# Float32 attention heads: exponential moved behind the transpose, maximum added in PSUM

## The chip, the cores and the metric

The kernel runs on one core of one Trainium2 chip. The metric is the device time of one execution in microseconds (us). Lower is better. Engines are named as in the profile: PE is TensorE's matmul stream, PEld its weight loads, DVE is VectorE, ACT is ScalarE, POOL is GpSimd, and SP issues most of the DMAs.

## What is computed

Attention for 8 batches of 8 heads (576 positions, 64 dimensions), followed by a gated feed-forward network over all 4608 tokens:

```
scores = scale * q @ k.T ; bias = -(cum[q] - cum[k]) with cum = cumsum(max(s, 0))
scores = where(causal, -1e9, scores + min(bias, 0))
scores = scores - max(scores) ; attn = exp(scores)
attn = attn / (sum(attn) + 1e-9) ; out = attn @ v
x = out as (4608, 512) ; gate = sigmoid(x @ w_gate) ; val = x @ w_val
y = (gate * val) @ w_out
```

q, k, v, s and the output are float32; the three weight matrices are float64.

## The kernel before

A head's 576 queries are cut into five tiles, numbered 0 to 4: tile 0 has 64 rows, the others 128, and tile t needs 64 + 128 t keys. A tile is one tick of the main loop, from tile 4 down to tile 0, so a head takes five ticks and there are 64 heads. The row maximum and the exponential work in two long SBUF buffers: `e_0` holds tiles 0, 1 and 2 (six blocks of 128 keys), `e_1` tiles 3 and 4 (nine blocks). There is one of each, so a tile of the next head may only be written when the same tile of this head has been read. The 64 columns behind a tile's keys are padding that later steps read.

The first eight heads (batch 0) run in float32 and their steps have names with `n_`. The other 56 run with operands split into two float16 parts (`s_part`, `max_part`, `p_part`, `av_part`) and have their probabilities transposed by DMA. A float32 tile goes through these steps:

- `n_s`: PE writes the scores to PSUM (L575), in two pieces for tile 4.
- `mask_part`: POOL masks the diagonal block in the bias row (L461).
- `n_max`: DVE adds the bias, negates, writes the sum to `e`, and takes the minimum (L584). The tile `em` receives it from an instruction that reads the accumulator. ACT then takes the exponential of the tile in place, from SBUF to SBUF, with `em` as bias (L587).
- `n_turn`: PE transposes blocks of `e` against the identity matrix, three to a PSUM bank `nt_ps` (L596). ACT copies each bank to the buffer `p16`, here used as float32 (L597). There are five banks to a head.
- `n_av`: PE multiplies the transposed probabilities by v and a column of ones (L605), DVE divides (L611 to L615), and after two heads `n_x` transposes the result (L629) and splits it into two float16 parts (L631, L632).

While these heads run, the feed-forward weights are prepared. A weight step takes 1024 values per partition of a float64 image (two 32-bit words each), decodes them (ACT L272, DVE L273, L274, L275), squares them (ACT L287), sums the squares over partitions (POOL L289), works out a power of two (DVE L125, L127), and writes high and low float16 parts (ACT L292, DVE L293). There are 18 such steps. The feed-forward matmuls (`ffn_in`, L657, and `ffn_out`, L687) start at tick 44 and go on, between the attention steps, until the end.

Each engine executes its own list in order. The lists are made by a scheduler with a timeline of its own; `first()` raises the priority of what it encloses. So an edit to one step also moves others in these lists.

Of the kernel before, what the change touches and what calls it, by code (L numbers as in the profile page):

```python
# [8 lines left out]
F32 = mybir.dt.float32  # L9
# [3 lines left out]
AF = mybir.ActivationFunctionType  # L13
ALU = mybir.AluOpType
ADD_REDUCE = bass.bass_isa.ReduceOp.add

P = 128
GT = 256
PSCALE = 2.0 ** 14
MASKED = 1.0e30  # L20
# [3 lines left out]
def tile_attention_then_gated_ffn(  # L24
# [11 lines left out]
    nc = tc.nc  # L36
# [10 lines left out]
    TILES = [(0, 64, 64)] + [(64 + 128 * i, 128, 192 + 128 * i) for i in range(4)]  # L47
    NTL = len(TILES)


    SETS = (((0, 1, 2), (0, 1, 3), 6), ((3, 4), (0, 4), 9))
    PAD = NTL * P - S
    NN = H
# [4 lines left out]
    wp = ctx.enter_context(tc.tile_pool(name="wp", bufs=2))  # L58
# [15 lines left out]
    e_s = [cp.tile([P, n * P], F32, name=f"e_{i}") for i, (_, _, n) in enumerate(SETS)]  # L74
# [4 lines left out]
    e_t, pf_t = {}, {}  # L79
# [3 lines left out]
            e_t[t] = e_s[i][:, cols]  # L83
            pf_t[t] = p_s[i].rearrange("p l n -> p (l n)").bitcast(F32)[:, cols]
    for t, (q0, m, w) in enumerate(TILES):
        nc.gpsimd.memset(e_t[t][:, w:], 0.0)
    ident = cp.tile([P, P], F32, name="ident")
    scrap = wp.tile([P, 2, NTL * P], F16, tag="x16", name="scrap", bufs=1).bitcast(F32)
    count, junk = scrap[:, 0, :P], scrap[:, 1, :P]
# [9 lines left out]
    for g in range(0, P, 32):  # L99
        nc.vector.tensor_scalar(ident[g : g + 32, g : g + 32], count[g : g + 32, :32], count[g : g + 32, 32:33], None,  # L100
                                ALU.is_equal)
    nc.gpsimd.memset(e_t[0][64:, :], 0.0)
    expo = cp.tile([P, 2], F32, name="expo")
    nc.gpsimd.memset(expo[:, 0:1], 460.75)
    nc.gpsimd.memset(expo[:, 1:2], 204.75)
# [13 lines left out]
    def first(now=True):  # L119
        return tc.high_priority(1000) if now else ExitStack()  # L120
# [355 lines left out]
    def p_part(i, h_):  # L476

        nc.scalar.activation(p_s[h_][:, 0], e_s[h_], AF.Copy, scale=PSCALE)  # L478
        ts, first_block, n = SETS[h_]
        flat = p_s[h_].rearrange("p l n -> p (l n)")  # L480
        for t, kb in zip(ts, first_block):
            if t:
                nc.vector.scalar_tensor_tensor(flat[:, LOW[t] * P : (LOW[t] + t) * P], e_t[t][:, : t * P], PSCALE,  # L483
                                               flat[:, kb * P : (kb + t) * P], ALU.mult, ALU.subtract)
        tails = [t + kb for t, kb in zip(ts, first_block)]
        e_ = e_s[h_].rearrange("p (b g n) -> p b g n", g=2, n=64)
        p_ = flat[:, : n * P].rearrange("p (b g n) -> p b g n", g=2, n=64)
        for bs in (tails[:2], tails[2:]):
            if bs:
                b = slice(bs[0], bs[-1] + 1, max(bs[-1] - bs[0], 1))  # L490
                nc.vector.scalar_tensor_tensor(p_[:, b, 1], e_[:, b, 0], PSCALE, p_[:, b, 0], ALU.mult, ALU.subtract)
        PT[i, h_] = wp.tile([P, 2 * n, P], F16, tag=f"pt{h_}", name=f"pt{h_}_{i}")
        m = n + sum(ts)
        nc.sync.dma_start_transpose(PT[i, h_][:, :m], flat[:, : m * P])
# [35 lines left out]
                                    x16.rearrange("p l n -> p (l n)"))  # L530


    qT, kT, nS, nA = {}, {}, {}, {}

    def n_load(p):
        b, h0 = divmod(2 * p, H)
# [39 lines left out]
            nS[i, t].append((ps, a, b_))  # L576

    def n_max(i, t):
        q0, m, w = TILES[t]
        init = MASKED  # L580
        r = rl[i]
        for n, (ps, a, b_) in enumerate(nS.pop((i, t))):
            acc = wp.tile([P, 1], F32, tag=f"em{n}", name=f"em{i}_{t}_{n}", bufs=3)
            nc.vector.tensor_tensor_reduce(e_t[t][:m, a:b_], ps[:m, : b_ - a], r[:m, a:b_], -1.0, init,  # L584
                                           ALU.add, ALU.min, acc[:m])
            init = acc[:m]
        nc.scalar.activation(e_t[t][:m, :w], e_t[t][:m, :w], AF.Exp, bias=init, scale=-1.0)  # L587

    def n_turn(i, t):

        h_, groups = {4: (1, (6,)), 3: (1, (3, 0)), 2: (0, (3,)), 1: (0, ()), 0: (0, (0,))}[t]
        o = p_s[h_].rearrange("p l n -> p (l n)").bitcast(F32)
        for a in groups:
            ps = pp.tile([P, 512], F32, tag="gv", name=f"nt_ps_{i}_{t}_{a}")
            for kb in range(3):
                nc.tensor.transpose(ps[:, kb * P : (kb + 1) * P], e_s[h_][:, (a + kb) * P : (a + kb + 1) * P], ident)  # L596
            nc.scalar.copy(o[:, a * P : (a + 3) * P], ps[:, : 3 * P])  # L597

    def n_av(i, t):
        p, j = divmod(i, 2)  # L600
# [140 lines left out]
    for n in range(nticks + 12):  # L741
        if n == NTL * EARLY:
            more_room()
        i, t = divmod(n, NTL)
# [10 lines left out]
        if 2 <= n < nticks + 2:  # L755
            a, z = divmod(n - 2, NTL)
            if a < NN:
                with first():
                    n_turn(a, NTL - 1 - z)
            elif z in (1, 4):  # L760
                p_part(a, 1 if z == 1 else 0)
        if 1 <= n < nticks + 1:
            a, z = divmod(n - 1, NTL)
            if a < NN:
                with first():
                    mask_part(a, NTL - 1 - z)
                    n_max(a, NTL - 1 - z)
            else:
                mask_part(a, NTL - 1 - z)
                max_part(a, NTL - 1 - z)  # L770
        if 3 <= n < 3 + NTL * NN:
            with first():
                a, z = divmod(n - 3, NTL)
# [113 lines left out]
        if n >= NE and state["u"] < 2 * NF:  # L887
            fdone = min(NF, int((n - NE + 1) * FPT))
            while state["u"] < 2 * fdone:
                f = state["u"]  # L890
# [17 lines left out]
        m = n - (11 if n > 2 * NTL * H + 30 else 7)  # L908
        b = m // (NTL * H) if m >= 0 else 0
        if b >= 1:  # L910
            r = m - b * NTL * H + 1
# [39 lines left out]
```

## Time and profile before

| | us |
|---|---|
| median of 3 runs | 1152.38 (1151.87 to 1155.03) |
| span of the profiled execution, first to last instruction | 1146.4 |
| what lies between that span and the median | 6.0 |
| PE busy over the span | 1091.6 (95%) |
| DVE busy | 776.1 (68%) |
| ACT busy | 749.5 (65%) |

The profiled execution shows its span but no time of its own; the median of the timed runs is put beside it instead. A busy time is the union of an engine's instructions, so shares of different engines overlap. The granted clock is the mean TensorE clock in a stretch, 1.00 being the higher of its two levels (2.4 GHz) and 0.50 the lower (1.2 GHz). A wait names the engine and line that ended the idle time before an instruction.

### The profile page before, as it was taken

What the parts mean: (1) busy time and instruction counts of PE and PEld (TensorE: products, weight loads), DVE (VectorE), ACT (ScalarE), POOL (GpSimd) and SP (SyncE); (2) the same over time, 40 slices, a digit from 0 to 9 for tenths busy, and PEclk for the clock granted to TensorE, in tenths of its full rate; (3) what the DMA queues carried; (4) which work ended last, traced back from release to release, by engine and by line L of the source; (5) the groups of instructions that cost most, each with busy time, mean ns of one, the idle gap of its engine ahead of it and who ended that gap; (6) DMA issues with size and microseconds to landing.
All of it is one profiled execution on the core that took longest, in us unless ns stands there. A gap on an engine that the chain in (4) does not pass through costs nothing.

```text
span 1146.4 us, 30336 instructions
## 1 busy us (share of the span) xinstructions
PE 1091.6 (95%) x11644; PEld 853.5 (74%) x11644; DVE 776.1 (68%) x2395; ACT 749.5 (65%) x1465; POOL 261.3 (23%) x568
## 2 busy tenths in 40 slices
PE   6787888989999999999999999999999999999998
PEld 4566676658767887788777777778877887787775
DVE  6899999866787777776565677777777775222222
ACT  6989778667777777676665577767776764233222
POOL 6634233222232222121211122212222221000000
PEclk9889899999999999999999999999999999999999
DMA  9676868995989888777646498868887774000000
GB/s 280 201 217 161 185 139 181 183 189 130 171 164 175 164 178 167 141 150 138 145 79 139 89 178 166 166 144 171 156 161 138 150 124 88 13 20 20 1 19 19
DMA packets 445518, 157.62 MB, mean 137 GB/s; under 512 B 403583, under 2 KB 435839, under 8 KB 445374
## 3 DMA queue, kind: packets, MB, share of 16 engines
q1 hardware_dynamic: 418686, 127.38, 57.6%
q10 hardware_dynamic: 23328, 17.04, 4.9%
q0 software_dynamic: 3360, 11.27, 3.0%
q8 instruction: 91, 1.49, 0.5%
q14 instruction: 53, 0.43, 0.1%
HBM read 56.92 MB, written 9.58 MB: 58 GB/s over the span
## 4 chain that ended last, share of the span: by engine, by line
PE 76%; DMA 7%; DVE 5%; issue 5%; ACT 5%; SPq 1%; POOL 1%; ACTq 0%; DVEq 0%; POOLq 0%
PE gv L657 42%; PE o L687 22%; PE s L447 3%; PE s L446 3%; DMA qk<-in_q_dram 1%; PE av L506 1%; PE av L508 1%; PE av L507 1%; DMA v<-in_v_dram 1%; DVE e L471 1%; PE s L575 1%; DMA pt<-p 1%; DMA T<-T 1%; PE na_ps L605 1%; DMA nqk<-in_q_dram 1%
## 5 line engine op out<-in xcount | busy, mean ns | idle before, releaser
L657 PE MATMUL gv<-x,w 128*128 128x256 f16 (+3 forms) x6912 | 613.2, 246 | 5.3 <-DVE t2f L664 2.7
L657 PEld LDWEIGHTS <-w 128*128 128x128 f16 x6912 | 533.8, 98 | 61.5 <-issue 5.2
L687 PE MATMUL o<-w2all,h 128*128 128x512 f16 x1296 | 314.8, 379 | 0.0
L461 POOL TENSOR_SCALAR_AFFINE_SELECT rl<-rl 128x64 f32<-128x64 f32 (+1 forms) x280 | 111.5, 399 | 519.7 <-DVE em L471 465.3
L474 ACT ACTIVATE e<-e,em 128x576 f32<-128x576 f32 x280 | 154.6, 554 | 92.3 <-DVE em L471 90.2
L687 PEld LDWEIGHTS <-h 128*128 128x128 f16 x1296 | 123.6, 98 | 108.7 <-issue 2.4
L662 ACT ACTIVATE th<-gv,scb 128x256 f32<-128x256 f32 (+3 forms) x288 | 111.4, 412 | 139.3 <-PE gv L657 138.4
L664 DVE SCALAR_TENSOR_TENSOR t<-th,gv 128x256 f32<-128x256 f32 x192 | 80.2, 417 | 133.5 <-ACT th L662 132.5
L471 DVE CUSTOM_DVE_ANT_0 e<-s,rl,qkcf 128x288 f32<-128x288 f32 x280 | 135.8, 485 | 30.5 <-PE s L447 24.9
L672 ACT ACTIVATE h<-t,hsc 128x256 f16<-128x256 f32 x192 | 96.6, 503 | 80.0 <-DVE t L664 80.0
L483 DVE SCALAR_TENSOR_TENSOR p<-e,p 128x384 f16<-128x384 f32 x224 | 102.0, 495 | 40.2 <-ACT p L478 39.4
L673 DVE SCALAR_TENSOR_TENSOR h<-t,hsc,h 128x256 f16<-128x256 f32 x192 | 93.2, 486 | 43.3 <-ACT h L672 42.8
L478 ACT ACTIVATE p<-e 128x1152 f16<-128x1152 f32 x112 | 112.1, 1001 | 2.8
L506 PE MATMUL av<-v,pt 128*128 128x65 f16 x560 | 68.0, 193 | 6.9 <-DMA pt<-p 6.9
L507 PE MATMUL av<-v,pt 128*128 128x64 f16 x560 | 68.0, 192 | 0.0
L446 PE MATMUL s<-T 128*128 128x288 f16 (+2 forms) x246 | 64.6, 280 | 3.6 <-DMA T<-qk 2.6
L508 PE MATMUL av<-v,pt 128*128 128x65 f16 x560 | 67.9, 194 | 0.0
L447 PE MATMUL s<-T 128*128 128x288 f16 (+2 forms) x246 | 62.2, 282 | 2.4 <-DMA T<-T 2.4
L506 PEld LDWEIGHTS <-pt 128*128 128x128 f16 x560 | 52.4, 97 | 13.6 <-DMA pt<-p 8.8
L706 POOL DMA_DIRECT2D out_dram<-osb x34 | 19.4, 570 | 174.6 <-ACT osb L705 173.8
L409 POOL PARTITION_BROADCAST cr<-cr x63 | 57.5, 913 | 6.1 <-DVE em L584 5.7
L455 DVE TENSOR_SCALAR rl<-cr,qkcf 128x576 f32<-128x576 f32 x56 | 29.1, 520 | 40.1 <-POOL cr L409 39.9
(157 smaller groups left out, 1436.9 us busy)
## 6 DMA issues: line engine op xcount, KB each, us to landing
v<-v SPq DMA_DIRECT2D x56, 162.5 KB
out_dram<-osb POOLq DMA_DIRECT2D x34, 256.0 KB, 2.9
v<-in_v_dram SPq DMA_DIRECT2D x64, 128.0 KB
T<-T SPq DMA_DIRECT2D x82, 72.0 KB
t2f<-in_v_dram SPq DMA_DIRECT2D x20, 288.0 KB
qk<-in_q_dram SPq DMA_DIRECT2D x17, 288.0 KB
qk<-in_k_dram SPq DMA_DIRECT2D x17, 288.0 KB
w2all<-in_moe_w_gate_dram ACTq DMA_DIRECT2D x7, 512.0 KB
```

The lines of the kernel that those rows point to most:

```text
L446: nc.tensor.matmul(ps[:, : b_ - a], lhs, T[i][:, 0, a:b_], start=True, stop=False)
L447: nc.tensor.matmul(ps[:, : b_ - a], lhs, T[i][:, 2, a:b_], start=False, stop=True)
L461: nc.gpsimd.affine_select(rl[i][:, q0:w], rl[i][:, q0:w], pattern=[[-1, m]], compare_op=ALU.is_ge, fill=-MASKED if i < NN else MASKED, bas ...
L471: nc.vector.tensor_tensor_reduce(e_t[t][:, a:b_], ps[:, : b_ - a], rl[i][:, a:b_], c, init, ALU.add, ALU.min, acc)
L474: nc.scalar.activation(e_t[t][:, :w], e_t[t][:, :w], AF.Exp, bias=init, scale=-1.0)
L478: nc.scalar.activation(p_s[h_][:, 0], e_s[h_], AF.Copy, scale=PSCALE)
L483: nc.vector.scalar_tensor_tensor(flat[:, LOW[t] * P : (LOW[t] + t) * P], e_t[t][:, : t * P], PSCALE, flat[:, kb * P : (kb + t) * P], ALU.m ...
L506: nc.tensor.matmul(AV[i][:, t], hi, v_[:, D : 2 * D + 1], start=kb == 0, stop=False)
L657: nc.tensor.matmul(ps[:, gv, a:e], w1[f][:, cc, gv, wl], x_of(b, cc)[:, xl, c0 + a : c0 + e], start=(c == 0), stop=(c == 3 * NC - 1))
L662: nc.scalar.activation(th[:, a:e], ps[:, 0, a:e], AF.Tanh, scale=scb[b][:, f : f + 1])
L672: nc.scalar.activation(h[:, 0], t2, AF.Copy, scale=hsc[:, f : f + 1])
L687: nc.tensor.matmul(ps[:m], h[:, hl, tt * P : tt * P + m], w2[f][:, wl], start=(f == 0 and c == 0), stop=(f == NF - 1 and c == 2))
```

## The change

In the float32 heads the sign is no longer turned while the bias is added: DVE takes the maximum of score plus bias over all 128 rows, and a further DVE instruction writes its negative to a tile `nm`. The in-place exponential is gone. PE transposes the block of raw sums and then, in the same PSUM group, adds a transposing matmul whose stationary operand is `nm` repeated over 128 columns, so that every column of the transposed block has its query's maximum subtracted. ACT then takes the exponential from PSUM where it copied before. The padding starts as minus 1e30, whose exponential is zero, and is set to zero after the last float32 head (`clear_pads`); the separate memset of the lower half of tile 0 goes.

```diff
-        nc.gpsimd.memset(e_t[t][:, w:], 0.0)
+        nc.gpsimd.memset(e_t[t][:, w:], -MASKED)
...
-    nc.gpsimd.memset(e_t[0][64:, :], 0.0)
...
+    tile_of = [[t for t, kb in zip(ts, first_block) for _ in range(t + 1)] for ts, first_block, _ in SETS]
+
+    def clear_pads():
+        for t, (q0, m, w) in enumerate(TILES):
+            nc.gpsimd.memset(e_t[t][:, w:], 0.0)
...
-        init = MASKED
+        init = -MASKED
...
-            nc.vector.tensor_tensor_reduce(e_t[t][:m, a:b_], ps[:m, : b_ - a], r[:m, a:b_], -1.0, init,
-                                           ALU.add, ALU.min, acc[:m])
-            init = acc[:m]
-        nc.scalar.activation(e_t[t][:m, :w], e_t[t][:m, :w], AF.Exp, bias=init, scale=-1.0)
+            nc.vector.tensor_tensor_reduce(e_t[t][:, a:b_], ps[:, : b_ - a], r[:, a:b_], 1.0, init,
+                                           ALU.add, ALU.max, acc)
+            init = acc
+        nmax[t] = wp.tile([P, 1], F32, tag="nm", name=f"nm{i}_{t}", bufs=4)
+        nc.vector.tensor_scalar(nmax[t], init, -1.0, None, ALU.mult)
...
-                nc.tensor.transpose(ps[:, kb * P : (kb + 1) * P], e_s[h_][:, (a + kb) * P : (a + kb + 1) * P], ident)
-            nc.scalar.copy(o[:, a * P : (a + 3) * P], ps[:, : 3 * P])
+                blk = ps[:, kb * P : (kb + 1) * P]
+                u = tile_of[h_][a + kb]
+                nc.tensor.matmul(blk, e_s[h_][:, (a + kb) * P : (a + kb + 1) * P], ident, start=True, stop=False,
+                                 is_transpose=True)
+                nc.tensor.matmul(blk, nmax[u].to_broadcast([P, P]), ident, start=False, stop=True, is_transpose=True)
+            nc.scalar.activation(o[:, a * P : (a + 3) * P], ps[:, : 3 * P], AF.Exp)
...
+                    if n == NTL * NN + 1:
+                        clear_pads()
```

The scheduler's lists change with it. On PE, the first transposes of head 1 (tile 4, bank `nt_ps_1_4_6`) stood together; the line numbers of the changed kernel are 4 to 8 higher here. Before:

```order
L575 MATMUL s1_0_0_432<-nk0_157,nq0_1_156 128x64
L596 MATMUL nt_ps_1_4_6_350<-ident_88,e_1_80 128x128 x3
L558 MATMUL nq_ps_1_1_1_391<-ident_88,nqk_1_229 128x96 x3
L596 MATMUL nt_ps_1_3_3_401<-ident_88,e_1_80 128x128 x3
L575 MATMUL s2_4_0_456<-nk1_371,nq1_0_369 128x288
```

The same place now:

```order
L602 MATMUL nt_ps_1_4_6_370<-ident_88,e_1_80 128x128
L579 MATMUL s1_1_0_423<-nk0_156,nq0_1_155 128x192
L604 MATMUL nt_ps_1_4_6_370<-ident_88,nm1_4_366 128x128
L602 MATMUL nt_ps_1_4_6_370<-ident_88,e_1_80 128x128
L604 MATMUL nt_ps_1_4_6_370<-ident_88,nm1_4_366 128x128
L602 MATMUL nt_ps_1_4_6_370<-ident_88,e_1_80 128x128
L604 MATMUL nt_ps_1_4_6_370<-ident_88,nm1_4_366 128x128
```

Each transpose is now followed by one that reads `nm`, and the group stands two score matmuls earlier in the list.

On DVE, the maximum of tile 4 of head 1 (two pieces, L584) and of tile 3 follow one another between weight steps (L293). Before:

```order
L584 ISA e_1_80,em1_4_1_345<-s1_4_288_309,cr1_186,em1_4_0_343 128x288
L584 ISA em1_4_1_345 128x1
L293 SCALAR_TENSOR_TENSOR w1_1_67<-w2all_78,wscale_111,w1_1_67 128x8x128
L584 ISA e_1_80,em1_3_0_358<-s1_3_0_333,cr1_186 128x448
L584 ISA em1_3_0_358 128x1
```

The same place now, where L273 is a weight step's instruction (L274 before):

```order
L587 ISA e_1_80,em1_3_0_381<-s1_3_0_349,cr1_185 128x448
L587 ISA em1_3_0_381 128x1
L273 SCALAR_TENSOR_TENSOR wa0_136<-wa0_136,w1_3_69 128x1024
L591 TENSOR_SCALAR nm1_3_383<-em1_3_0_381 128x1
L587 ISA e_0_79,em1_2_0_444<-s1_2_0_368,cr1_185 128x320
```

The negation stands not directly behind the maximum but behind one instruction of a weight step.

On ACT, the split of the first float16 head (`qk16_8`, whose transfer feeds head 8) stood among the exponentials of head 7. Before:

```order
L597 COPY p16_0_81<-nt_ps_6_2_3_1100 128x384
L587 ACTIVATE e_1_80<-e_1_80,em7_4_1_1156 128x576
L387 ACTIVATE qk16_8_1121<-qk32_4_981,qksc4_1092 96x6x64
L389 ACTIVATE qk16_8_1121<-qk32_4_981,qksc4_1092 96x6x64
L292 ACTIVATE w2all_78<-wa0_137,wscale_111 128x1024
```

The same pair now (L271 belongs to a weight step):

```order
L271 ACTIVATE wa0_136<-t2f_134 128x1024
L605 ACTIVATE p16_1_82<-nt_ps_6_3_0_1202 128x384
L386 ACTIVATE qk16_8_1256<-qk32_4_1097,qksc4_1223 96x6x64
L388 ACTIVATE qk16_8_1256<-qk32_4_1097,qksc4_1223 96x6x64
L605 ACTIVATE p16_0_81<-nt_ps_6_2_3_1231 128x384
```

It stands one bank of head 6 earlier, ahead of everything of head 7. From about the middle of head 18 on, the lists of all engines are the same as before.

## Rows read from the trace of the kernel before

**Rows 1.** Page, part 2: busy tenths in 40 slices of the span.

```profile
PE   6787888989999999999999999999999999999998
PEclk9889899999999999999999999999999999999999
```

**Rows 2.** Windows: busy us and instructions of each engine, granted clock, DMA share, GB/s.

```profile
200.00:300.00 100.00, 91.06 (x1059) 67.77 (x1058) 71.29 (x234) 67.87 (x135) 22.51 (x50) 1.00 0.86 170
300.00:600.00 300.00, 298.19 (x3534) 236.28 (x3532) 220.53 (x717) 212.17 (x423) 67.30 (x161) 1.00 0.76 150
600.00:900.00 300.00, 300.00 (x3289) 234.50 (x3287) 219.60 (x720) 208.04 (x404) 67.55 (x160) 1.00 0.77 150
```

**Rows 3.** Windows of the first 200 us: PE, PEld, DVE, ACT, POOL busy, clock.

```profile
20.00:66.00 46.00, 36.43 (x224) 29.70 (x223) 37.47 (x99) 44.52 (x90) 26.78 (x42) 0.83 0.78 235
66.00:110.00 44.00, 34.65 (x221) 26.54 (x219) 41.39 (x105) 40.32 (x74) 20.64 (x33) 0.97 0.66 179
110.00:120.00 10.00, 9.50 (x46) 7.92 (x45) 6.95 (x17) 5.92 (x12) 0.39 (x1) 0.52 0.64 144
120.00:200.00 80.00, 68.52 (x712) 55.69 (x709) 74.45 (x229) 65.13 (x120) 27.77 (x49) 0.98 0.84 173
```

**Rows 4.** Waits of DVE, 20 to 120 us: releaser, total us, times, longest.

```profile
DVE xe_w L125 <- POOL wtot L289: 4.9, 4, 2.4
DVE w L273 <- ACT w2all L272: 2.2, 2, 1.9
DVE w L293 <- ACT w L292: 1.2, 2, 1.0
DVE qk L388 <- ACT qk L387: 0.9, 1, 0.9
```

**Rows 5.** Waits of POOL, 20 to 120 us.

```profile
POOL wtot L289 <- ACT w2all L287: 9.4, 2, 7.9
POOL wtot L289 <- ACT w L287: 8.7, 7, 1.9
```

**Rows 6.** Groups on ACT, 0 to 130 us, then two forms: busy, mean ns | idle.

```profile
L587 ACT ACTIVATE e<-e,em 128x576 f32<-128x576 f32 (+4 forms) x40 | 22.1, 563 | 2.0 <-DVE em L584 1.9
L597 ACT COPY p<-nt_ps 128x384 f32<-128x384 f32 x40 | 18.4, 476 | 1.8 <-PE nt_ps L596 1.5 <-issue 0.3
...
L587 ACT ACTIVATE e<-e,em 128x448 f32<-128x448 f32 x8 | 5.4, 672 | 0.6 <-DVE em L584 0.6
L587 ACT ACTIVATE e<-e,em 128x320 f32<-128x320 f32 x8 | 4.6, 574 | 0.5 <-DVE em L584 0.5
```

**Rows 7.** DVE: forms (0 to 125 us), then two instructions in order of time.

```profile
L125 DVE TENSOR_SCALAR xe_w<-wtot 128x1 int32<-128x1 int32 x14 | 2.0, 146 | 5.2 <-POOL wtot L289 5.1
...
L584 DVE CUSTOM_DVE_ANT_0 e<-s,cr 128x192 f32<-128x192 f32 x8 | 2.8, 353 | 1.0 <-POOL cr L461 1.0
...
L584 DVE CUSTOM_DVE_ANT_0 e<-s,cr 64x64 f32<-64x64 f32 x8 | 1.7, 211 | 0.7 <-POOL cr L461 0.3
...
43.71 0.14 DVE L127 TENSOR_SCALAR wscale<-xe_w 128x1 int32<-128x1 int32 x1
43.77 0.51 DVE L584 CUSTOM_DVE_ANT_0 e<-s,cr,em 128x288 f32<-128x288 f32 x1
```

**Rows 8.** Timeline of PE: transposes at the higher and at the lower clock.

```profile
16.46 0.82 PE L596 MATMUL nt_ps<-ident,e 128*128 128x128 f32 x6
36.67 0.28 PE L596 MATMUL nt_ps<-ident,e 128*128 128x128 f32 x1
52.20 0.42 PE L596 MATMUL nt_ps<-ident,e 128*128 128x128 f32 x1
58.83 1.54 PE L596 MATMUL nt_ps<-ident,e 128*128 128x128 f32 x6 [0.70 <-ACT p L597]
```

**Rows 9.** Chain that ended last, first and last of four: start, us, what.

```profile
58.83 1.54 PE nt_ps L596 x6
...
65.07 1.08 PE s L575 x2
```

More of the change, by code (lines that the diff above doesn't have):

```diff
@@ L530, in split_x @@
                                     x16.rearrange("p l n -> p (l n)"))
-    qT, kT, nS, nA = {}, {}, {}, {}
+    qT, kT, nS, nA, nmax = {}, {}, {}, {}, {}
+    tile_of = [[t for t, kb in zip(ts, first_block) for _ in range(t + 1)] for ts, first_block, _ in SETS]
+    def clear_pads():
+        for t, (q0, m, w) in enumerate(TILES):
+            nc.gpsimd.memset(e_t[t][:, w:], 0.0)
     def n_load(p):
@@ L578, in n_max @@
     def n_max(i, t):
-        q0, m, w = TILES[t]
-        init = MASKED
+        init = -MASKED
         r = rl[i]
```

## The prediction

> **What bounds the kernel now.** I read the slices first, then the windows, the waits and the groups. From the seventh slice on PE is busy nine tenths or more [rows 1], 298 of 300 us and then 300 of 300 [rows 2]. There PE is the bound and runs the same list before and after. A microsecond gained or lost ahead of it goes through to the end; nothing else does. So what counts is how long the first 200 to 300 us take, and in those the float32 heads fill about 10 to 120.
>
> In 20 to 120 us, the first three of the windows in [rows 3], no engine is full all the time. ACT is busy 44.52 + 40.32 + 5.92 = 90.8 us, of which 20 to 66 is nearly solid (44.5 of 46). DVE is busy 85.8, with 14.2 idle, and is the tighter one from 66 to 110 (41.4 of 44). PE is busy 80.6, with 19.4 idle. From 120 to 200 DVE leads with 74.5 of 80. I take DVE as the ruler, since it is close to full before and after 120, and ask which of its gaps the change can close. Its waits [rows 4] say which end on ACT: 2.2 and 1.2 directly, 0.9 for head 8's split, and 4.9 through POOL's sum over partitions, which itself waits 8.7 + 9.4 us for ACT's squares [rows 5]. That is 9.2 of the 14.2 us.
>
> **The change part by part.**
>
> *ACT.* It loses 40 exponentials, 22.1 us busy [rows 6]. The 40 copies of 476 ns become 40 exponentials of 384 columns from PSUM, which no row shows. Lower bound: the copy's 476 ns, plus 0. Upper bound: the old exponential with its `em` operand, between its 320 and 448 column forms, (574 + 672) / 2 = 623 ns, 5.9 us in all. I take a quarter, 1.5 us, since shape, source and destination are the copy's and the operand `em` is gone. ACT goes from 90.8 to about 70 us in the stretch.
>
> *DVE.* It gains 40 instructions on 128x1. Such a one shows 146 ns, but the next starts 0.06 us after it [rows 7]. So 40 cost between 2.4 and 5.8 us; as the stream around them is dense, I take 0.075 each, 3.0 us. Tile 0's eight maxima now cover 128 rows: between 0 and 1.1 us (8 x 0.142, the step to the next form in [rows 7]); taken as 0, as the columns stay. The negation stands behind one weight instruction and PE waits for it there. Behind that wait stand score matmuls of the next tiles. Before, the transposes waited for an exponential in ACT's full list, so I add nothing.
>
> *PE.* It gains 120 transposes with weight loads. At the higher clock six take 0.82 us and one alone 0.28, so one more costs (0.82 - 0.28) / 5 = 0.108 us; at the lower, (1.54 - 0.42) / 5 = 0.224 us [rows 8]. That bounds the sum at 13.0 and 26.9 us. The granted clock, weighted over the three windows, is 0.86 [rows 3], so 28% of the stretch lies at 0.50; the mean cost is 0.14 and the sum 16.9 us. It goes into 19.4 us of PE idle time. I cost it at nothing on the path; the cover is 2.5 us thin, and what lies beyond it is the third case below.
>
> The rows show transposes at both clocks, in runs where other matmuls stand around them, and can't say whether a transpose helps to raise the clock. The Trainium skill, on its page "TensorE: Matmul & The Clock Gate", Part 4, says that transpose mode doesn't count as PE-busy in the same way and that the full clock doesn't engage for it. By that the added work would cost its upper bound; by the rows' mixture it costs the middle value. No row here settles it.
>
> *POOL.* One memset goes and five small ones move behind head 7. In 110 to 120 us POOL is busy 0.39 us [rows 3]; the float16 steps of head 8 that read the padding come later in every list. Cost 0, as that idle time hides them.
>
> *Order.* Head 8's split stands earlier on ACT, ahead of all of head 7, so its transfer starts earlier; the 0.9 us wait on it is in the 9.2.
>
> *Sum.* ACT sheds more than 20 us where DVE lost 9.2 us to it. A shorter list does not close every gap: the first one of 2.4 us also holds POOL's sum. Bounds are 0 and 9.2; I take five sixths, 7.7 us. Less 3.0 for the negations this leaves 4.7 us. Against the profiled execution that is a span of 1146.4 - 4.7 = 1141.7; with the 6.0 us that lie between its span and the median, 1147.7.
>
> **The rivals.**
>
> *PE takes ACT's place.* After the change PE is busy about 97.5 of 100 us in the stretch if the stretch keeps its length. In-order lists seldom reach that: DVE would then wait for scores as it waited for ACT. Against it: the transposes stand where PE waited anyway. Recovered 3.0, paid 3.0: 1152.4.
>
> *The transposes run at the lower clock.* If they draw the clock down, or leave it down as in 110 to 120 us (0.52), they cost 26.9 us, and PE's idle time holds only 19.4. It decides from 0.162 us for each (19.4 / 120), above the 0.14 of the mixture. The excess is 7.5 us; DVE's share is hidden under it: 1159.9. The page's rule above would lead here. For it: PE already ran at 0.83 in 20 to 66 with fewer transposes. Against it: six transposes ran at the higher clock at 16.46 us, and 66 to 110 kept 0.97 with just as many to a head.
>
> *The clock comes up.* From 58.83 to 66.15 the chain lies on PE at the lower clock [rows 9]. If denser PE work keeps it at the higher, half of these 7.3 us goes too: 4.7 + 3.7 = 8.4 less, 1144.0.
>
> **How the numbers follow.** A difference under 0.3%, 3.5 us, can't be told from none here. Forecast 0.42, with a range of its own from 1145.5 to 1150 that follows from recovering 9.2 or 5.4 us; PE in ACT's place 0.28; lower clock 0.22; higher clock 0.08. The edge of 0.3% is 1148.9, which leaves 0.08 of the forecast on the side of no change. So faster 0.34 + 0.08 = 0.42, same 0.08 + 0.28 = 0.36, slower 0.22. The range from 1143 to 1159 takes in the three likelier cases but for the upper half of the lower-clock case, and most of the fourth.
>
> **What would show it.** On ACT, the line of the in-place exponential is gone and the 40 from PSUM have a mean between 476 and 623 ns. DVE's 40 negations add about 3 us of busy time. The waits of DVE for ACT and for POOL's sum in the head stretch fall from 9.2 to about 2 us, and no wait of DVE for PE of like size appears. PE's busy time in the stretch rises by about 17 us and its idle time falls to a few. Head 8's first maximum comes some 5 us earlier, and the lag stays the same to the end. I am wrong if the added transposes have a spacing above 0.16 us, if DVE waits for scores, or if the gain is there at 120 us and is lost by 250, where transfers and PE meet.

## The result

| | median us | range, executions | mean granted clock (median) |
|---|---|---|---|
| before | 1153.87 | 1151.87 to 1155.60, 5 | 0.979 to 0.981 (beside the experiments) |
| changed | 1158.71 | 1156.42 to 1159.28, 5 | 0.984 |

The ratio is 1.0043, interval 1.0029 to 1.0058: about 5 us slower. Run again beside the last experiments, the changed kernel came to 1.0054 (1.0035 to 1.0073). The forecast was 1147.7, faster. Every ratio below is to the kernel before, run beside the experiment.

Single executions of one kernel differ by several us (before: 1146.98 to 1160.23 over 30 executions), so a profile is one draw. Below, sums and verdicts go by medians and ratios; profiles show where things stand.

### The profile page after: what moved, and what is told of

It reads as the page before. It is cut to its first block, busy times and chain, and to the rows that moved or that the text cites. A ratio compares the mean times of both kernels' runs of the same rounds, so it can differ in the third digit from the quotient of the medians.

```text
span 1156.9 us, 30566 instructions
## 1 busy us (share of the span) xinstructions
PE 1104.2 (95%) x11764; PEld 866.6 (75%) x11764; DVE 778.6 (67%) x2435; ACT 732.4 (63%) x1425; POOL 266.6 (23%) x572
## 4 chain that ended last, share of the span: by engine, by line
PE 80%; DMA 7%; DVE 4%; issue 3%; ACT 2%; POOL 1%; SPq 1%; DVEq 0%; ACTq 0%; POOLq 0%
PE gv L665 44%; PE o L695 23%; PE s L446 3%; PE s L445 3%; DMA qk<-in_q_dram 1%; PE av L507 1%; PE av L505 1%; DMA v<-in_v_dram 1%; PE av L506 1%; PE na_ps L613 1%; PE s L579 1%; DMA T<-T 1%; DMA w2all<-in_moe_w_val_dram 1%; DMA T<-qk 1%; PE av L509 1%
## 5 line engine op out<-in xcount | busy, mean ns | idle before, releaser
L695 PE MATMUL o<-w2all,h 128*128 128x512 f16 x1296 | 314.8, 379 | 0.8 <-ACT h L680 0.8
L460 POOL TENSOR_SCALAR_AFFINE_SELECT rl<-rl 128x64 f32<-128x64 f32 (+1 forms) x280 | 114.7, 411 | 544.5 <-DVE em L470 488.6
L695 PEld LDWEIGHTS <-h 128*128 128x128 f16 x1296 | 123.0, 98 | 106.8 <-ACT h L680 1.0
L470 DVE CUSTOM_DVE_ANT_0 e<-s,rl,qkcf 128x288 f32<-128x288 f32 x280 | 135.7, 486 | 30.4 <-PE s L446 25.7
L445 PE MATMUL s<-T 128*128 128x288 f16 (+2 forms) x246 | 65.5, 281 | 4.7 <-DVE em L470 4.5
L446 PE MATMUL s<-T 128*128 128x288 f16 (+2 forms) x246 | 63.9, 281 | 5.5 <-DMA T<-T 5.4
L505 PEld LDWEIGHTS <-pt 128*128 128x128 f16 x560 | 52.6, 98 | 11.0 <-DMA pt<-p 5.9
L506 PEld LDWEIGHTS <-pt 128*128 128x128 f16 x560 | 52.7, 97 | 4.9
```

The lines of the kernel that those rows point to most:

```text
L445: nc.tensor.matmul(ps[:, : b_ - a], lhs, T[i][:, 0, a:b_], start=True, stop=False)
L446: nc.tensor.matmul(ps[:, : b_ - a], lhs, T[i][:, 2, a:b_], start=False, stop=True)
L460: nc.gpsimd.affine_select(rl[i][:, q0:w], rl[i][:, q0:w], pattern=[[-1, m]], compare_op=ALU.is_ge, fill=-MASKED if i < NN else MASKED, bas ...
L470: nc.vector.tensor_tensor_reduce(e_t[t][:, a:b_], ps[:, : b_ - a], rl[i][:, a:b_], c, init, ALU.add, ALU.min, acc)
L505: nc.tensor.matmul(AV[i][:, t], hi, v_[:, D : 2 * D + 1], start=kb == 0, stop=False)
L506: nc.tensor.matmul(AV[i][:, t, 0:D], hi, v_[:, 0:D], start=False, stop=False)
```

## The profile after

Engine totals and busy tenths in 40 slices, from the page of the changed kernel.

```profile
PE 1104.2 (95%) x11764; PEld 866.6 (75%) x11764; DVE 778.6 (67%) x2435; ACT 732.4 (63%) x1425; POOL 266.6 (23%) x572
...
PE   6897688999999999999999999999999999999998
...
PEclk9997798999999999999999999999999999999999
```

From the eighth slice on PE is busy nine tenths or more; in [rows 1] it is so from the tenth. Up to there the clock row has changed: nine tenths or more in the first three slices, then two slices at 7.

Groups of single lines: duration in ns (least, median, most), first and last start in us.

```profile
L605 ACT ACTIVATE p<-nt_ps x40: 463/491/502, 16.4 to 123.8; 128x384 f32<-128x384 f32 x40
L591 DVE TENSOR_SCALAR nm<-em x40: 106/145/155, 12.8 to 115.2; 128x1 f32<-128x1 f32 x40
L604 PE MATMUL nt_ps<-ident,nm x120: 272/273/477, 13.4 to 119.0; 128*128 128x128 f32 x120
L470 DVE CUSTOM_DVE_ANT_0 e<-s,rl,qkcf x280: 258/512/686, 114.8 to 974.2; 128x288 f32<-128x288 f32 x28, 128x320 f32<-128x320 f32 x28, 128x64 f32<-128x64 f32 x28, 128x448 f32<-128x448 f32 x28
L286 ACT ACTIVATE w2all<-wa x6: 1040/1042/1057, 109.6 to 208.7; 128x1024 f16<-128x1024 f32 x6
```

The exponential from PSUM takes 491 ns, 15 above the copy it replaces [rows 6]. L470 first starts at 114.8 us: head 8's first maximum. The last row holds six of the weight squares, and the last of them starts at 208.7 us. The same two rows of the kernel before, from a second profile of it (experiment 4):

```profile
L471 DVE CUSTOM_DVE_ANT_0 e<-s,rl,qkcf x280: 267/510/685, 119.1 to 966.9; 128x288 f32<-128x288 f32 x28, 128x320 f32<-128x320 f32 x28, 128x64 f32<-128x64 f32 x28, 128x448 f32<-128x448 f32 x28
...
L287 ACT ACTIVATE w2all<-wa x6: 1043/1057/1061, 100.9 to 176.5; 128x1024 f16<-128x1024 f32 x6
```

So head 8 is 4.3 us earlier after the change and the last weight square 32.2 us later. Read together, these two rows say that the new lists bring heads forward and push weight steps back. What that costs shows later. In both profiles head 18 starts at about the same time (its first maximum at 264.5 us, 263.8 before), but by then the changed kernel has done fewer of the `ffn_out` matmuls (L695, L687 before), which need the weights of `w_out`. Their busy time and number on PE (then on PEld) up to head 18, and from there to head 20, changed kernel first, then before:

```profile
0.00:264.50 264.50, 22.64 (x96) 8.83 (x96) 0.93 0.80 188
264.50:309.00 44.50, 18.25 (x78) 7.33 (x78) 1.00 0.68 132
```

```profile
0.00:263.80 263.80, 35.27 (x144) 14.31 (x144) 0.94 0.79 189
263.80:300.50 36.70, 7.29 (x30) 2.85 (x30) 1.00 0.82 167
```

By head 20 both have done 174. The 48 that the changed kernel had left over take 11.0 us more of PE there (18.25 less 7.29), and head 20 starts 8.5 us later than before.

Windows of the changed kernel, to be held against [rows 2, 3]:

```profile
20.00:66.00 46.00, 39.99 (x302) 34.26 (x301) 40.17 (x124) 38.00 (x75) 28.74 (x45) 1.00 0.81 248
66.00:110.00 44.00, 34.54 (x240) 28.92 (x239) 37.35 (x106) 30.63 (x54) 19.25 (x26) 0.91 0.59 163
110.00:120.00 10.00, 9.47 (x62) 8.68 (x61) 7.48 (x29) 5.47 (x10) 4.68 (x13) 0.71 0.98 209
120.00:200.00 80.00, 61.69 (x609) 48.64 (x609) 67.84 (x198) 56.15 (x97) 25.05 (x44) 0.87 0.79 155
200.00:300.00 100.00, 96.72 (x1017) 70.65 (x1015) 75.03 (x244) 72.71 (x147) 26.07 (x52) 1.00 0.79 160
```

To 66 us DVE and PE are busier than before and the clock is full. From 66 to 110 DVE falls from 41.39 to 37.35. From 120 to 200 all three fall, DVE from 74.45 to 67.84 and PE from 68.52 to 61.69: no engine is full there.

ACT and its queue from 81 to 91 us: start, duration, what, and in brackets the idle time before it and its releaser.

```profile
81.84 0.55 ACTq L252 DMA_DIRECT2D t2f<-in_moe_w_out_dram  x1
82.43 0.79 ACTq L259 DMA_DIRECT2D t2f<-in_moe_w_out_dram  x1
83.32 1.06 ACT L286 ACTIVATE w<-wa 128x1024 f16<-128x1024 f32 x1 [1.01 <-POOL cr L460]
83.37 3.97 ACTq L252 DMA_DIRECT2D ws<-in_moe_w_out_dram  x1
84.28 0.19 ACT L286 ACTIVATION_READ_ACCUMULATOR w<-wa 128x1 f32 x1
87.38 2.28 ACTq L259 DMA_DIRECT2D ws<-in_moe_w_out_dram  x1
89.71 0.84 ACT L356 ACTIVATE jq<-qk 96x768 f16<-96x768 f32 x1 [5.25 <-issue]
90.46 0.19 ACT L356 ACTIVATION_READ_ACCUMULATOR jq<-qk 96x1 f32 x1
90.56 1.04 ACT L286 ACTIVATE w<-w2all 128x1024 f16<-128x1024 f32 x1
```

Four loads of `w_out` stand close together on ACT's list, with a square between the pairs. The first two are issued in 0.55 and 0.79 us, the next two in 3.97 and 2.28 us, and ACT stands still for 5.25 us with "issue" as the reason. The square behind them starts at 90.56. The kernel before has slow issues too, but ACT had work at hand while they ran, and stood still for 0.24 us:

```profile
84.16 1.47 ACTq L260 DMA_DIRECT2D t2f<-in_moe_w_out_dram  x1
...
89.46 2.59 ACTq L260 DMA_DIRECT2D t2f<-in_moe_w_out_dram  x1
...
93.72 1.16 ACT L272 ACTIVATE wa<-t2f 128x1024 f32<-128x1024 f32 x1 [0.24 <-issue]
```

Back in the changed kernel, the waits of DVE, then of PE, from 20 to 120 us, show whom that reaches:

```profile
DVE xe_w L124 <- POOL wtot L288: 8.9, 4, 4.8
DVE nm L591 <- PE nt_ps L604: 0.9, 1, 0.9
```

```profile
PE s L579 <- DVE em L587: 5.6, 3, 4.5
PE nt_ps L604 <- DVE nm L591: 3.9, 5, 1.5
```

The sum over partitions waits for the square, DVE for the sum (4.8 us at once), and PE for DVE's maximum behind it (4.5 us at once). The waits of DVE that were to fall from 9.2 to 2 us are at 8.9 on this one line.

## The experiments

Two theories. **Order**: the loss is that of the lists that the scheduler wrote anew. **Work**: the added transposes find no idle time on PE. To part them, a kernel needs the new work in the old lists. In some experiments each engine's list was therefore taken from a built kernel and pinned, with an edge without a semaphore from each instruction to the next on its engine:

```
+    rows = list(tc.nc.cur_bb.bb.instructions)
+    for steps in ORDER:            # one list per engine
...
+            tc.add_manual_dep(rows[at], before, _dep(), reason="order")
```

**1. New work, old order.** The lists of before, with L604 behind each L602, the negation behind its maximum, and no in-place exponential. It also has six `nm` buffers in place of four.

> The changed kernel's instructions, in the lists of the kernel before: each engine's order of before is written out and pinned; the second transposing matmul stands directly behind its first, each negation directly behind its maximum, the five clearing memsets where POOL had them after the change (and the negated maxima have 6 buffers in place of 4, since the old order holds more of them at once). Order theory (the loss of 4.8 us comes from the order that the scheduler wrote anew, with the w_out loads bunched on ACT's list): the loss is gone, 1147 to 1154 us. Work theory (the 120 added transposes, 13 us of PE, find no idle time to go into): the loss stays, 1157 to 1161 us.

Measured: 1149.60 us, ratio 0.9976 (0.9960 to 0.9993). The order theory holds. The same work is 0.24% faster than before in one order and 0.43 to 0.54% slower in another. ACT's loads and the squares in its profile:

```profile
83.46 0.63 ACTq L256 DMA_DIRECT2D ws<-in_moe_w_out_dram  x1
84.12 0.68 ACTq L263 DMA_DIRECT2D ws<-in_moe_w_out_dram  x1
89.32 0.55 ACTq L256 DMA_DIRECT2D t2f<-in_moe_w_out_dram  x1
89.93 0.65 ACTq L263 DMA_DIRECT2D t2f<-in_moe_w_out_dram  x1
...
L290 ACT ACTIVATE w2all<-wa x6: 1044/1053/1057, 107.1 to 184.4; 128x1024 f16<-128x1024 f32 x6
```

No load takes over 0.68 us to issue here, and the last square starts at 184.4 us in place of 208.7 (176.5 before). This profile is of an execution of 1153.60 us, 4.0 above the median.

**2. Old work, each transpose twice, old order.**

```
                 nc.tensor.transpose(blk, e_s[h_][:, (a + kb) * P : (a + kb + 1) * P], ident)
+                nc.tensor.transpose(blk, e_again, ident)
```

> The kernel before with each of its 120 transposes in the float32 heads issued twice, in its own order written out and pinned; nothing else differs, the exponential stays in place. Work theory: PE's added 13 us go to the end for a large part, 1158 to 1167 us. Order theory: they lie in PE's idle time, 1153 to 1156 us.

Measured: 1154.64 us, ratio 1.0023 (1.0004 to 1.0043). About 2.7 us of 13 go to the end (0.5 to 5.0), so most of the work does find room, or is given back; experiments 7 and 12 take that up.

**3. New order, one transpose.**

```
-                nc.tensor.matmul(blk, e_s[h_][:, (a + kb) * P : (a + kb + 1) * P], ident, start=True, stop=False,
-                                 is_transpose=True)
-                nc.tensor.matmul(blk, nmax[u].to_broadcast([P, P]), ident, start=False, stop=True, is_transpose=True)
+                nc.tensor.transpose(blk, e_s[h_][:, (a + kb) * P : (a + kb + 1) * P], ident)
```

> The changed kernel without its second transposing matmul (the exponentials are of scores from which no maximum is taken; the negations stay and are read by nothing), scheduled anew. Work theory: the 13 us of PE go, 1146 to 1154 us. Order theory: as the scheduler bunches the w_out loads again, 1156 to 1160 us.

Measured: 1159.80 us, ratio 1.0071 (1.0047 to 1.0095). 13 us of PE work are gone and nothing is gained. The work theory falls here. Its lists were scheduled anew and differ from the changed kernel's in many places, so it prices the second transpose in no fixed order; experiment 7 does.

**4. Before again.**

> The kernel before, unchanged, for a second profile of it. Both theories expect a time between 1151.9 and 1155.6 us, a span 1.5 to 2 us below the time of its own execution, and PE idle for some 55 us.

Measured: 1151.57 us with a span of 1149.6, 2.0 apart; the time lies 0.3 below the range that I gave. The prediction had assumed 6.0 us between span and median. With 2.0 us, the profiled execution with its span of 1146.4 took about 1148.4, some 4 to 5.5 us under the median: a short one.

**5. New order, loads spread.** The changed kernel's lists, pinned, with two pairs of rows on ACT moved.

```
 ACT: ... W286 #9, DMA, DMA, turn 29, [-DMA w_out, -DMA w_out,] W286 #10, [-DMA w_out, -DMA w_out,] jq,
      W286 #11, W291 #9, W291 #10, turn 30, jq, W291 #11, [+DMA, +DMA,] turn 31, [+DMA, +DMA,] L271 #12 ...
```

> The changed kernel in its own lists, written out and pinned, but for two pairs of rows on ACT: the two w_out loads that stood behind the 29th turn and the two behind the tenth square are issued later, the one pair behind the third decoded rest of the next step, the other behind the 31st turn, so that no four stand together. Bunch theory (ACT is held while it issues four loads in a row, 3.97 and 2.28 us in the profile after at 83 to 90 us): 3 to 6 us below the changed kernel, 1149 to 1154 us. Late-weights theory (the new lists put the weight steps from the twelfth on behind the heads, so that the first gated pieces and head 18 start late): nothing changes there, 1156 to 1160 us.

Measured: 1154.71 us, ratio 1.0012 (0.9995 to 1.0028), 0.7 above the range of the bunch theory, but 0.31 to 0.42% under the changed kernel by four rows moved. In its profile the four are issued in 0.55 to 1.97 us, and no idle time of ACT is put down to them:

```profile
86.20 1.04 ACT L290 ACTIVATE w<-w2all 128x1024 f16<-128x1024 f32 x1
...
88.31 0.55 ACTq L256 DMA_DIRECT2D ws<-in_moe_w_out_dram  x1
88.90 0.68 ACTq L263 DMA_DIRECT2D ws<-in_moe_w_out_dram  x1
...
89.65 0.87 ACTq L256 DMA_DIRECT2D t2f<-in_moe_w_out_dram  x1
...
90.55 1.97 ACTq L263 DMA_DIRECT2D t2f<-in_moe_w_out_dram  x1
```

The first row is the square that stood behind the loads: 86.20 us in place of 90.56, 4.4 us earlier, against 3.6 to 4.8 gained by the ratios. In time the four loads still start within 2.3 us of each other, so that four stand together can't be the whole condition. They come 5 to 8 us later here, behind that square.

**6. New order, late weight steps under the heads' priority.**

```
+                with first():
                     while f == 8 and wnext["step"] < NF + 1:
                         weight_step()
                     while f >= NF and wnext["step"] < min(f + NF + WLA, len(wsteps)):
                         weight_step()
```

> The changed kernel with the weight steps that the first gated pieces call for (from the ninth piece on) traced under the heads' priority, and scheduled anew: on ACT seven tanh rows stand ahead of head 8's twelfth exponential row where three stood. The four w_out loads still stand within eight rows. Late-weights theory: 1149 to 1155 us, the span's part up to head 21 shrinks by 4 to 8 us. Bunch theory: 1156 to 1160 us.

Measured: 1156.29 us, ratio 1.0027 (1.0008 to 1.0046). That lies in the range of the bunch theory, and by itself it is not told apart from the changed kernel, whose intervals overlap it. In its profile two of the four loads still take 4.32 and 2.16 us to issue.

**7. Old order, one transpose.** Experiment 1 without L604, so that no maximum is subtracted.

> The new work in the old order (as in the first experiment) without the second transposing matmul; the exponentials are of scores from which no maximum is taken. It prices that matmul where the order is held. If its 120 instructions, 13 us, lie in PE's idle time: the first experiment's 1149.6 us, within 1.5. If a fifth of them goes to the end, as in the second experiment (2.7 us): 1145.5 to 1148 us. If all: 1137 us.

Measured: 1156.58 us, ratio 1.0020 (0.9999 to 1.0040). All three expectations missed: taking 13 us of PE work out made the kernel slower, by 0.44%. The mean granted clock fell with it, from 0.9875 to 0.976 (medians of 12 executions each).

**8. Old work, 40 negations added.**

```
+        nc.vector.tensor_scalar(nmax[t][:m], init, -1.0, None, ALU.mult)
         nc.scalar.activation(e_t[t][:m, :w], e_t[t][:m, :w], AF.Exp, bias=init, scale=-1.0)
```

> The kernel before in its own order, pinned, with 40 negations of the maxima added on VectorE that nothing reads. The prediction's term: 3.0 us more, 1155 to 1156.5 us beside a before of 1152.8. If they lie in VectorE's idle time: within 1.5 us of before.

Measured: 1154.64 us, ratio 1.0014 (0.9997 to 1.0031): 1.6 us, between nothing and 3.6. It decides neither way.

**9. The changed kernel again.**

> The changed kernel, unchanged, on the same chip as the three that follow, to hold them against it. Both theories: 1.0029 to 1.0058 of before, 1156 to 1159.5 us, and a mean granted clock of 0.980 to 0.986 over its executions.

Measured: 1158.20 us, ratio 1.0054 (1.0035 to 1.0073), clock 0.985. In its profile the two late loads take 4.31 and 2.33 us to issue; the bunch is not an accident of one execution.

**10. Old order, three transposes.** One more transpose ahead of each pair of experiment 1.

> The new work in the old order, with the first transpose of each block issued once more ahead of the two: 120 more transposes, some 13 us of PE, same results. Clock theory (more PE work in the heads lifts the granted clock of that stretch, which gives back what the work costs; without the second matmul the mean clock over 12 executions was 0.976 and the time 1156.6 us, with it 0.9875 and 1149.6): the mean clock is 0.988 or more and the time no higher than 1151 us. Work theory (each further 120 cost some 2.7 us): 1151.5 to 1156 us, clock within 0.002 of 0.9875.

Measured: 1156.42 us, ratio 1.0035 (1.0018 to 1.0051), clock 0.991. The clock rose as the clock theory said, the time did not follow: 0.59% over experiment 1. What the second transposes give back, the third do not. Both theories miss, the work theory by 0.4 us and by the clock.

**11. Weights first and loads spread.** The lists of experiment 6, pinned, with the loads moved as in 5.

> The lists of the sixth experiment (late weight steps under the heads' priority), pinned, with the two pairs of w_out loads on ACT moved apart as in the fifth. If the bunch costs 3.6 us (1158.7 less the fifth experiment's 1154.7, by ratios 1.0043 less 1.0012) and the late weights another 1.8 (the sixth's 1.0027), and the two add: 1151 to 1153.5 us. If the two shares overlap: 1154 to 1156.5 us.

Measured: 1150.99 us, ratio 0.9998 (0.9982 to 1.0015). That is at the lower edge of the range for shares that add. Together they are 0.45 to 0.56%, the whole loss; by how much the weight steps add to the loads is within the noise (1.0012 against 0.9998, the intervals overlap). Squares in its profile:

```profile
L290 ACT ACTIVATE w2all<-wa x6: 1040/1056/1058, 101.0 to 181.5; 128x1024 f16<-128x1024 f32 x6
```

**12. Old order, zeros added.** Experiment 1 with all its instructions, but zeros in place of the negated maxima.

```
-        nc.vector.tensor_scalar(nmax[t], init, -1.0, None, ALU.mult)
+        nc.vector.tensor_scalar(nmax[t], init, 0.0, None, ALU.mult)
```

> As the first experiment (new work, old order, both transposing matmuls), but the negation multiplies by 0, so that the second matmul adds zeros and the exponentials are those of the seventh experiment. Clock theory (it is the work on PE that counts): as the first, 1147.5 to 1151.5 us with a mean clock of 0.985 to 0.989. Values theory (the unshifted exponentials themselves made the seventh slow): as the seventh, 1154 to 1158.5 us and 0.974 to 0.979.

Measured: 1149.24 us, ratio 0.9976 (0.9954 to 0.9997), clock 0.987. It equals experiment 1 and not 7, so the work on PE counts and not the values. Windows of experiment 7, then of 12, whose profile is of a long execution (1155.54 us):

```profile
20.00:66.00 46.00, 37.12 (x233) 31.99 (x232) 40.58 (x113) 36.20 (x69) 22.99 (x41) 0.85 0.79 236
66.00:110.00 44.00, 35.26 (x184) 28.29 (x183) 37.42 (x108) 29.91 (x52) 12.21 (x29) 0.77 0.59 163
120.00:200.00 80.00, 70.69 (x658) 57.73 (x658) 70.95 (x211) 61.38 (x110) 22.13 (x48) 0.89 0.76 160
```

```profile
20.00:66.00 46.00, 39.28 (x290) 33.98 (x289) 41.22 (x119) 38.25 (x74) 22.07 (x43) 0.96 0.81 244
66.00:110.00 44.00, 37.71 (x219) 31.00 (x218) 37.12 (x107) 28.21 (x49) 11.61 (x28) 0.81 0.54 151
120.00:200.00 80.00, 67.04 (x649) 55.65 (x649) 69.14 (x206) 60.09 (x107) 21.67 (x46) 0.92 0.72 156
```

In all three windows the clock is higher with the added transposes: 0.96 for 0.85, 0.81 for 0.77, 0.92 for 0.89. In the first, PE does 57 instructions more for 2.2 us more of busy time.

## Why the prediction was wrong

**The step that failed is the order.** The prediction read the lists of the changed kernel at head 8, saw the heads moved forward, took that as a gain of some 5 us and had the lag "stay the same to the end". At 115 us the gain is there: 4.3 us. What had been moved back to make room was put at nothing. Held by experiment 1, the new order costs 0.67 to 0.78%, 7.7 to 9.0 us (1.0043 and 1.0054 less 0.9976). One part of it is shown: the `w_out` loads in a bunch hold ACT (experiment 5: 0.31 to 0.42%). The other is the weight steps behind the heads. The profiles show what they push back, the 48 `ffn_out` matmuls; in the medians, calling for the weights earlier with the bunch gone is worth another 0.14%, which is within the noise. Experiment 11, with both mended, is back at the time of before; 0.22% still part it from experiment 1, and what makes those is not settled (experiment 1 also had more `nm` buffers).

Single profiles, each with the time of its own execution, show where it is lost. A head's column is the start of its first maximum, in us.

| profile | execution | head 8 | head 18 | `ffn_out` matmuls by head 18 | head 20 |
|---|---|---|---|---|---|
| before (experiment 4) | 1151.57 | 119.1 | 263.8 | 144 | 300.5 |
| changed | 1158.71 | 114.8 | 264.5 | 96 | 309.0 |
| experiment 5, loads spread | 1151.66 | 110.2 | 257.5 | 96 | 302.1 |
| experiment 11, weights first too | 1147.78 | 114.1 | 262.8 | 144 | 294.8 |
| experiment 1, old order | 1153.60 | 126.8 | 269.6 | 144 | 303.6 |

The loads cost the heads time early, and the postponed matmuls cost it between heads 18 and 20. Head 8 says little about the end: it comes 7.7 us later than before in experiment 1, whose median is the lower of the two.

**The rule "what counts is how long the first 200 to 300 us take" held.** From head 20, at 295 to 309 us, to the end of the execution it is 848.5 to 853.5 us in all thirteen profiles behind the prediction. The warning "the gain is there at 120 us and is lost by 250" is close to what happened: it is lost at 264.5 us (0.7 behind), and most of the loss follows up to 309.

**ACT.** The exponential from PSUM came to 491 ns, inside 476 to 623. Busy time fell by 17.1 us over the whole kernel (749.5 to 732.4). But "DVE's waits fall from 9.2 to 2 us" failed, and with it the 7.7 us of the sum. The part that ended on ACT directly did fall, from 4.3 to 1.0 us. The part through POOL's sum rose from 4.9 to 8.9, of which the longest, 4.8, stands behind the bunch; without the bunch (experiment 5) it is 5.2, and in the old order (experiment 1) 5.6. So the old order didn't relieve DVE of it either.

**DVE.** 3.0 us for 40 negations; experiment 8 measured 1.6 (-0.3 to 3.6), which does not contradict it. Nothing was added for PE waiting on the negation: such waits (L604 for L591) come to 3.9 us in the changed kernel's profile. What they cost at the end is not shown.

**PE.** PE's busy time rose by 12.6 us (1091.6 to 1104.2) for 120 instructions, 0.105 each, at the lower bound of 0.108 and not the mixture's 0.14; against the second profile of before (1094.5) it is 9.7. From 20 to 120 us it rose by 3.4 us and not 17, and 16.0 us stay idle, not "a few". So the cover was wider than the prediction had it. "Costed at nothing on the path" was wrong in both directions: 2.7 us in the old work (experiment 2), and a gain of 0.44% in the new (7 against 12).

**The rivals.** "PE takes ACT's place" (1152.4) and "the transposes run at the lower clock" (1159.9) give times near to what came, by other ways: DVE's maxima wait for scores for 0.2 us only, PE is idle more and not less from 120 to 200, and the clock is at 1.00 in 20 to 66 (though at 0.91 from 66 to 110, below the 0.97 of before). That the range up to 1159 held 1158.71 is luck, since its upper part was there for the lower clock. The Trainium skill, "TensorE: Matmul & The Clock Gate", Part 4, by which transposes don't count as busy for the clock in the same way, would have led to the 1159.9. The runs disagree with the rule, since the same lists run at 0.976 without the second transposes and at 0.987 with them, and the second transposes themselves take 273 ns in the median, as at the higher clock [rows 8]. "The clock comes up" had 0.08. Its premise, that more PE work keeps the clock up, is what the runs show (experiments 7, 12 and 10); its time of 1144.0 is not.

**The sum in the right order.** Experiment 1 has the work that the prediction priced, and gained 0.24%, 2.8 us of the 4.7 forecast. That the numbers are near is luck: DVE's idle time from 20 to 120 us is 12.6 in its profile, against 14.2 [rows 3], and head 8 does not come earlier but 7.7 us later. Where the gain arises is not shown, as the one profile is of an execution longer than before's. The parts don't add. ACT's relief with the negations but one transpose: +0.20% (experiment 7). The second transpose without the relief: +0.23% (experiment 2). Both: -0.24%.

**Two slips in the working.** PE is busy nine tenths or more from the tenth slice on, not the seventh [rows 1]. And the forecast's lower edge of 1145.5 does not follow from recovering 9.2 us with 3.0 paid, which gives 1146.2.

**The version to keep** is experiment 1: 0.9976 of before (0.9960 to 0.9993) and some 0.7% under the changed kernel. With its interval ending at 0.9993, it is faster, if by little; experiment 12, the same instructions, came to the same ratio (0.9954 to 0.9997).

## What to carry to other kernels

Where a scheduler writes the lists, an edit is two changes: the work and the order. Cost the second too: follow what is moved back, not only what is moved forward, and look for DMA issues that end up side by side on a compute engine's list. Read a gain where the engine that bounds the rest has done the same work in both versions (here head 20), not at the first milestone. To measure an edit by itself, pin the old lists and put the edit into them; and before any cover is counted as idle time on PE, ask which clock that idle time leaves behind.

## What the runs showed of the hardware

- **More transposes, higher clock.** With 120 transposes taken out, the mean granted clock was 0.976 (new work, old order); with them 0.987; with 120 more on top 0.991. In the new order, where the lists changed too, it was 0.9735 and 0.985. Of the two levels, 1.2 and 2.4 GHz, the lower then holds for 2 x (1 - clock) of the time: 55 us of 1156.6 at 0.976, 30 us of 1149.2 at 0.987. Work at the lower level takes twice as long (0.224 for 0.108 us for one more transpose [rows 8]), so 25 us less of it give back up to 12.7 us of PE's time, about what the transposes cost. That the kernel gained 5 us more is not explained by this sum, so that the clock makes the whole difference is not shown. From 0.9875 to 0.991 it is 29 to 21 us, up to 4 given back for 13, and the kernel lost 6.8.
- **Issuing a load can hold an engine.** A `w_out` load takes 0.55 to 0.68 us of ACT's queue in most issues, and 3.97 and 2.28 (again 4.31 and 2.33) as third and fourth within 6 us. ACT's own instructions behind it wait meanwhile (5.25 us, again 5.63). Four within 6.5 us can also pass at 0.68 or less (experiment 1), so their number alone does not decide; what fills up was not measured.
- **An accumulating transpose in float32** shows 273 ns (median of L604, from start to end, with the next one overlapping), and 120 of them added 0.08 to 0.105 us each to PE's busy time (against the two profiles of before), no more than plain ones cost at the higher clock [rows 8].
